# Hourglass attention with a ReGLU layer on one Trainium2 core: gate layer of chunks 2 to 5 in seven half products, in a new written order

## The chip, the cores and the metric

The kernel runs on one core of a Trainium2 chip. The core has engines that run their own instruction queues in order and meet at semaphores: TensorE (PE, matmuls, with weight loads shown apart as PEld), VectorE (DVE), ScalarE (ACT), GpSimd (POOL), and SyncE (SP), which here only starts transfers. The metric is the device time of one execution in microseconds (us). Before the change the median of three runs is 349.23 (348.65 to 349.43).

## The reference

Attention comes in two parts that are added, for 8 batches, 8 heads, 576 positions and head dimension 64; then a gated feed-forward layer follows, for 4608 tokens of 512 numbers, with 1536 inner columns:

```python
q_d, k_d, v_d = (t.reshape(B, H, S // 4, 4, D).mean(axis=3) for t in (q, k, v))
out = np.repeat(sm_attn(q_d, k_d, v_d), 4, axis=2)         # pooled 4:1
mask = np.abs(pos[:, None] - pos[None, :]) < 4
out += softmax(np.where(mask, scale * q @ k.T, -1e9)) @ v  # local band
x = out.transpose(0, 2, 1, 3).reshape(B * S, H * D)
y = (np.maximum(x @ w_gate, 0.0) * (x @ w_val)) @ w_out
```

## The kernel before

**Tiles.** The 64 heads are 32 head pairs, four to a batch; a pair fills the 128 partitions. Attention writes its output transposed into xT (four rows of 4608 columns in each partition, a row for each group of 128 of the 512 features). The feed-forward layer takes the tokens in 9 chunks of 512. A chunk's gate and value layers have 12 column blocks of 128 each; a block is four matmuls of 128x512 (emit_h_mm, L848), one for each row of xT, into one PSUM bank. ACT applies relu to a gate block (L857, into a ring r1 of three), and DVE multiplies it with the value block in PSUM (L860) into gT. PSUM has eight banks of 2 KB a partition, 512 numbers.

**The output layer in seven products.** The output layer of a chunk is done in two units of 256 tokens (class Unit, L904). A unit is a 2x2 block product in Strassen and Winograd's form: sums of blocks of gT on DVE (sums, L927, four of them, "next" being their low part and "sumhi" the high part), prepared combinations of weights (wt, L899), and seven products p/1 to p/7 of six matmuls of 128x256 each (mm, L933). Products accumulate in three PSUM regions a, b and d; ACT copies a out between them (keep, L967), and c11, c12, c22 on DVE and c21 on ACT give the results. p/7 adds to the region a, which keep/2 reads.

**Periods.** In the period of chunk c, the PE does the attention of four head pairs, the gate and value layers of chunk c, and the two units of chunk c-1. For a pair, the steps are the pooled and banded scores (L733, L737), exp on ACT (L746, L751), the mask on DVE (L759), denominators and numerators on PE (L764, L779, L784), the logarithm and the inverse on ACT (ln L796, inv L817), the normalization on DVE (xn, L799; L658 for early pairs), and the sum into xT (xsum, L803; L662 for early pairs). For pairs to come, q and k are loaded by POOL's DMAs (L365) and transposed by SP's (L426), keys are copied into block form on ACT (kk L696, kd L703), and keys and queries are pooled by DVE (pool, L433).

**The order is written by hand.** Each engine's queue has its instructions in the order of a list of tokens. A token names a step, its argument, its half period u, and its chunk: hg is a gate block, hv a value block, relu and gate what follows. FRONT covers the start and chunks 0 and 1; ORDER is one period, run for chunks 2 to 5 (emit_periods, L1299; "<" and ">" mean the chunk before or after); MAIN covers chunk 6, and then chunks 7 and 8, whose gate and value layers are also done in seven products: class Seven (L1081), its matmuls (product, L1094), copies (L1105) and finishing steps (L1110 on DVE, L1112 on ACT), the sums of weights (L1070) and of x (L1079), and a gate step that takes the maximum with zero itself (L1166). In chunks 2 to 5 the gate and value blocks use two pairs of PSUM banks in turn, 0 to 3, which they share with the units; attention has banks 4 to 7.

Of the kernel before, what the change touches and what calls it, by code (L numbers as in the profile page):

```python
# [9 lines left out]
FP32 = mybir.dt.float32  # L10
# [7 lines left out]
FRONT = """  # L18
pads loadk/0 loadv/0 loadq/1 loadk/1 loadv/1 loadq/2 cast tr/0/2/4 loadk/2 ev/0/20V/4 tr/0/1/3 tr/0/0/2
ev/0/21V/4 ev/0/10A/3 vd/0/6 loadv/2 ev/0/11A/3 ev/0/01A/2 ev/0/00A/2 loadq/3 warm/5/6 tr/1/0/7 vc/0/6  # L20
s1/0/2 ev/1/00A/7 loadk/3 tr/1/2/1 ed/0/2 tr/1/1/0 ev/1/20V/1 ev/1/11A/0 loadv/3 sd/0/6 ev/1/21V/1
ev/1/10A/0 rd/0/6 ex/0/0/2 td/0/6 wg/0 brief/16/2 vd/1/6 ev/1/01A/7 warm/2/7 ma/0/0 ex/0/1/2 s1/1/0 wv/0
ma/0/1 ed/1/0 ones/4 su/0/4 ex/1/1/0 ru/0/4 loadq/4 ex/1/0/0 tu/0/0/4 warm/5/7 tr/2/1/2 tr/2/2/3 tu/0/1/4
ev/2/11A/2 tr/2/0/0 ev/2/10A/2 loadk/4 ev/2/21V/3 xp/0/0/4 ev/2/20V/3 ev/2/01A/0 xp/0/1/5 ev/2/00A/0
ma/1/0 loadv/4 vc/1/6 warm/1/7 s1/2/0 ma/1/1 xe/0/0A/4 xe/0/1V/5 sd/1/6 ex/2/1/0 ones/5 su/1/4 rd/1/6
td/1/6 ed/2/0 ru/1/4 warm/3/7 vd/2/6 loadq/5 tu/1/1/4 ex/2/0/0 tr/3/1/2 tu/1/0/4 tr/3/2/3 loadk/5 vc/2/6
tr/3/0/0 ev/3/20V/3 ev/3/10A/2 xp/1/1/5 sd/2/6 ev/3/21V/3 loadv/5 ev/3/01A/0 xe/1/1V/5 xp/1/0/4
ev/3/00A/0 ma/2/0 ev/3/11A/2 ma/2/1 xe/1/0A/4 s1/3/0 wg/1 rd/2/6 su/2/4 td/2/6 ed/3/0 ru/2/4 ex/3/0/0
tu/2/1/4 hv/0/0/7 wv/1 hv/0/1/7 tu/2/0/4 ex/3/1/0 vd/3/6 ma/3/0 ones/6 warm/4/1 const/0 const/1 xp/2/1/5
vc/3/6 xp/2/0/4 ma/3/1 sd/3/6 xe/2/1V/5 xe/2/0A/4 loadq/6 tr/4/0/0 rd/3/6 su/3/4 td/3/6 tr/4/1/2 loadk/6  # L30
ru/3/4 hv/1/0/1 ev/4/11A/2 tu/3/0/4 hg/0/0/6 ev/4/10A/2 hg/0/1/6 tu/3/1/4 loadv/6 tr/4/2/3 ev/4/01A/0
ev/4/00A/0 xp/3/1/5 ev/4/21V/3 ev/4/20V/3 xp/3/0/4 wg/2 hv/0/2/7 xe/3/1V/5 xe/3/0A/4 hg/1/0/0 s1/4/2 wv/2
hv/0/3/7 ex/4/0/2 hv/1/1/1 loadq/7 hg/1/1/0 hg/1/2/0 ed/4/2 ma/4/0 hv/1/2/1 hg/0/2/6 hg/0/3/6 ex/4/1/2
hg/1/3/0 hv/1/3/1 relu/0/6 tr/5/0/2 ma/4/1 tr/5/1/3 loadk/7 relu/1/0 tr/5/2/4 den/4/1/5 ev/5/20V/4 vd/4/6
ev/5/10A/3 hg/3/*/0 ev/5/21V/4 gate/0/7 vc/4/6 ev/5/00A/2 gate/1/1 hg/2/*/6 ev/5/11A/3 loadv/7 ev/5/01A/2
relu/3/0 den/4/0/4 relu/2/6 hv/2/*/7 wg/3 ln/4 num/4/0/2 wv/3 gate/2/7 tr/6/1/0 inv vd/5/1 num/4/1/3
loadq/8 s1/5/4 vc/5/1 xn/2 hv/3/*/1 ex/5/0/4 ev/6/11V/0 ed/5/4 ma/5/0 hg/4/*/2 gate/3/1 ex/5/1/4 loadk/8
tr/6/0/4 relu/4/2 ma/5/1 tr/6/2/1 hg/5/*/6 ev/6/20V/1 ev/6/00A/4 ev/6/01V/4 ev/6/10A/0 ev/6/21V/1
den/5/0/4 xsum/4 wo/0 den/5/1/5 num/5/0/2 ln/4 hv/4/*/3 wo/1 inv hv/5/*/7 gate/4/3 wo/2 relu/5/6 hg/6/*/0
gate/5/7 qk/b0/0@0 num/5/1/3 zero/b/5 relu/6/0 vd/6/1 xn/2 s1/6/4 vc/6/1 tr/7/1/0 ex/6/1/4 hv/6/*/1  # L40
ed/6/4 qk/b1/0@0 ma/6/1 hg/7/*/2 ex/6/0/4 hg/8/*/6 ma/6/0 relu/7/2 gate/6/1 qk/b2/0@0 tr/7/0/4 num/6/0/2
ev/7/01V/4 ev/7/00A/4 den/6/1/5 tr/7/2/1 qk/b3/0@0 ev/7/10A/0 den/6/0/4 ev/7/20V/1 hv/7/*/3 relu/8/6
ev/7/21V/1 xsum/5 wo/3 ln/4 hv/8/*/7 gate/7/3 inv vd/7/1 ev/7/11V/0 gate/8/7 num/6/1/3 zero/b/6 vc/7/1
hg/9/*/0 loadv/8 xn/2 s1/7/4 relu/9/0 xsum/6 hg/10/*/2 ex/7/0/4 wt/0 v/b/0@0 ex/7/1/4 hv/10/*/3 ma/7/0
relu/10/2 ma/7/1 hv/9/*/1 ed/7/4 gate/10/3 qk/a0/1@0 hg/11/*/0 gate/9/1 qk/a1/1@0 next/0/1@0 den/7/0/4
relu/11/0 tr/8/1/2 qk/a2/1@0 den/7/1/5 flip/9 zero/k/0 ev/8/11V/2 tr/8/2/3 ev/8/10A/2 next/1/1@0 tr/8/0/0
qk/a3/1@0 hv/11/*/1 ln/4 ev/8/01V/0 ev/8/20V/3 v/a/1@0 ev/8/21V/3 inv num/7/0/6 gate/11/1 num/7/1/7
zero/b/0 p/1/0@1 qk/b0/1@0 ev/8/00A/0 sumhi/0/0@1 xn/6 p/2/0@1 keep/1/0@1 qk/b1/1@0 vd/8/1 xsum/7
scores/a/0@1 vc/8/1 qk/b2/1@0 sumhi/1/0@1 wt/1 vd/9/1 exp/a1/0@1 hg/0/0@1 qk/b3/1@0 ed/a/0@1 c11//0@1
v/b/1@0 sum/2/0@1 p/6/0@1 vc/9/1 relu/0/0@1 wt/2 p/5/0@1 v4/b/1@0 exp/a0/0@1 flip/10 hv/0/0@1 mask/a1/0@1  # L50
keep/2/0@1 qk/a0/0@1 mask/a0/0@1 p/7/0@1 gate/0/0@1 o/a00/0@1 sum/3/0@1 keep/3/0@1 o/a01/0@1 qk/a1/0@1
o/a10/0@1 ln/a0/0@1 o/a11/0@1 c22//0@1 hg/2/0@1 zero/b/1 wt/3 qk/a2/0@1 ln/a1/0@1 p/3/0@1 qk/a3/0@1
pool/b/0@1 inv/a/0@1 p/4/0@1 v/a/0@1 hv/2/0@1 c21//0@1 c12//0@1 v4/a/0@1 relu/2/0@1 xn/a0/0@1 hg/1/0@1
xn/a1/0@1 hv/1/0@1 relu/1/0@1 qk/b0/0@1 flip/11 xsum/a/0@1 scores/b/0@1 gate/1/0@1 hg/3/0@1 exp/b1/0@1
qk/b1/0@1 next/0/0@1 exp/b0/0@1 qk/b2/0@1 hg/4/0@1 mask/b1/0@1 ed/b/0@1 mask/b0/0@1 qk/b3/0@1 hv/3/0@1
next/1/0@1 tn/1/0@1 v2/b/0@1 v4/b/0@1 relu/3/0@1 gate/2/0@1 relu/4/0@1 o/b00/0@1 o/b01/0@1 gate/3/0@1
o/b10/0@1 ln/b0/0@1 o/b11/0@1 vd/10/0 pool/a/0@1 v/b/0@1 p/1/1@1 ln/b1/0@1 hg/5/0@1 inv/b/0@1 flip/12
hv/5/0@1 qk/a0/1@1 keep/1/1@1 xn/b1/0@1 qk/a1/1@1 p/6/1@1 xn/b0/0@1 zero/b/2 zero/v/0 hv/4/0@1 qk/a2/1@1
keep/2/1@1 next/2/0@1 vc/10/0 zero/d/0 qk/a3/1@1 scores/a/1@1 relu/5/0@1 gate/4/0@1 p/7/1@1 v/a/1@1
exp/a0/1@1 gate/5/0@1 p/2/1@1 exp/a1/1@1 mask/a0/1@1 hg/0/1@1 ed/a/1@1 mask/a1/1@1 xsum/b/0@1 keep/3/1@1  # L60
qk/b0/1@1 o/a00/1@1 relu/0/1@1 o/a01/1@1 c11//1@1 o/a10/1@1 o/a11/1@1 next/3/0@1 tn/3/0@1 v1/a/1@1
v2/a/1@1 v4/a/1@1 flip/13 p/4/1@1 ln/a1/1@1 qk/b1/1@1 pool/b/1@1 p/5/1@1 ln/a0/1@1 hg/2/1@1 inv/a/1@1
c22//1@1 hv/0/1@1 c21//1@1 xn/a0/1@1 hg/1/1@1 xn/a1/1@1 zero/b/3 zero/v/1 const/2 p/3/1@1 relu/1/1@1
gate/0/1@1 qk/b2/1@1 scores/b/1@1 c12//1@1 hg/3/1@1 qk/b3/1@1 exp/b1/1@1 xsum/a/1@1 exp/b0/1@1 flip/14
mask/b1/1@1 qk/a0/0@2 hv/1/1@1 ed/b/1@1 mask/b0/1@1 tm/b/1@1 v1/b/1@1 v2/b/1@1 v4/b/1@1 qk/a1/0@2
hv/2/1@1 gate/1/1@1 relu/3/1@1 kk/a0/1@1 kk/a1/1@1 pool/a/1@1 relu/2/1@1 o/b00/1@1 o/b01/1@1 o/b10/1@1
ln/b0/1@1 o/b11/1@1 hv/3/1@1 v/b/1@1 ln/b1/1@1 hg/5/1@1 gate/3/1@1 qk/a2/0@2 inv/b/1@1 kd/a0/1@1
kd/a1/1@1 gate/2/1@1 zero/d/1 hg/4/1@1 xn/b1/1@1 hv/4/1@1 relu/4/1@1 xn/b0/1@1 zero/b/4 zero/v/2 zero/k/1
relu/5/1@1 qk/a3/0@2 hv/5/1@1 xsum/b/1@1 qk/b0/0@2 qk/b1/0@2 qk/b2/0@2 qk/b3/0@2 v/a/0@2 v/b/0@2
"""  # L70
MAIN = """
fl/31 o:scores/a/0@6 o:gate/5/1@5 o:p/1/0@6 o:exp/a0/0@6 o:gate/4/1@5 o:hg/0/0@6 o:sumhi/0/0@6 o:ed/a/0@6
o:mask/a0/0@6 o:p/2/0@6 o:relu/0/0@6 o:kk/b0/0@6 o:kk/b1/0@6 o:sumhi/1/0@6 o:next/0/1@5 o:o/a00/0@6
o:keep/1/0@6 o:o/a01/0@6 o:o/a10/0@6 o:next/1/1@5 o:o/a11/0@6 o:hg/2/0@6 o:pool/b/0@6 o:ln/a0/0@6
o:p/6/0@6 o:c11//0@6 o:hv/0/0@6 o:sum/2/0@6 o:keep/2/0@6 o:inv/a/0@6 o:kd/b0/0@6 o:kd/b1/0@6 o:sum/3/0@6
o:p/5/0@6 o:relu/2/0@6 o:after/3/0@6 o:v1/a/0@6 o:v2/a/0@6 o:v4/a/0@6 o:xn/a0/0@6 o:p/7/0@6 o:hg/4/0@6
o:keep/3/0@6 o:p/4/0@6 o:next/0/0@6 o:c22//0@6 o:scores/b/0@6 o:gate/0/0@6 o:c21//0@6 o:p/3/0@6
o:exp/b0/0@6 o:next/1/0@6 o:hv/2/0@6 o:c12//0@6 o:ed/b/0@6 o:mask/b0/0@6 o:tm/b/0@6 o:v1/b/0@6 o:v2/b/0@6
o:v4/b/0@6 oy/0/0 o:hg/1/0@6 o:gate/2/0@6 o:o/b00/0@6 o:o/b01/0@6 o:next/3/0@6 o:relu/1/0@6 o:o/b10/0@6
o:o/b11/0@6 o:pool/a/0@6 o:hv/1/0@6 o:ln/b0/0@6 o:hv/4/0@6 o:gate/1/0@6 o:inv/b/0@6 o:kd/a0/0@6  # L80
o:kd/a1/0@6 o:kk/a1/0@6 o:hg/3/0@6 o:xsum/a/0@6 o:relu/4/0@6 o:kk/a0/0@6 o:xn/b0/0@6 o:hv/3/0@6
o:relu/3/0@6 o:p/1/1@6 o:hg/5/0@6 wv/0 o:keep/1/1@6 o:gate/3/0@6 o:scores/a/1@6 o:relu/5/0@6 o:p/6/1@6
o:next/2/0@6 o:exp/a0/1@6 o:gate/4/0@6 o:hg/0/1@6 o:mask/a0/1@6 o:tm/a/1@6 o:v1/a/1@6 o:v2/a/1@6
o:v4/a/1@6 o:keep/2/1@6 o:hv/5/0@6 o:ed/a/1@6 o:kk/b0/1@6 ws/0 o:relu/0/1@6 o:p/7/1@6 o:gate/5/0@6
o:o/a00/1@6 o:o/a01/1@6 o:xsum/b/0@6 o:keep/3/1@6 o:kk/b1/1@6 o:o/a10/1@6 o:o/a11/1@6 o:ln/a0/1@6
o:hg/2/1@6 o:pool/b/1@6 o:p/2/1@6 o:inv/a/1@6 o:kd/b0/1@6 o:kd/b1/1@6 o:p/4/1@6 o:c11//1@6 o:hv/0/1@6
o:xn/a0/1@6 o:c21//1@6 o:p/5/1@6 o:hg/1/1@6 o:c22//1@6 ws/2 oy/1/1 o:scores/b/1@6 o:relu/1/1@6 oy/0/1
o:p/3/1@6 o:gate/0/1@6 o:exp/b0/1@6 o:hg/3/1@6 o:mask/b0/1@6 o:ed/b/1@6 o:hv/2/1@6 o:relu/2/1@6
# [49 lines left out]
ORDER = """  # L138
# [1262 lines left out]
```

## Time and profile before

| | |
|---|---|
| median of three runs | 349.23 us (349.23, 349.43, 348.65) |
| the profiled execution | 348.82 us |
| its span in the trace | 347.1 us |
| granted clock of TensorE, mean | 1.00 |
| busy: DVE / ACT / POOL | 270.1 / 257.4 / 184.0 us |
| periods of chunks 2, 3, 4, 5 | 37.60, 36.06, 36.06, 35.40 us |

The span is the time between the first and the last instruction that the profiler shows; the execution's own time is 1.7 us longer. A group of instructions is written as line, engine, operation, output <- input, shapes and count, then busy time, mean duration in ns, and the idle time just ahead with what ended it. In a timeline a row is start, duration, and what ran, with the idle time ahead in brackets. Durations overlap in a stream: a matmul's row of 379 ns and the next one's start 216 ns after its own. The marks of the periods are the starts of the first pair's pooled scores.

### The profile page before, as it was taken

How to read it: one execution, taken by the hardware profiler on the slowest of the kernel's cores; microseconds unless marked ns; L12 is line 12 of the kernel's file. 1: busy time of each engine (PE TensorE's matmuls, PEld its weight loads, DVE VectorE, ACT ScalarE, POOL GpSimd, SP SyncE). 2: the span in 40 equal slices, each digit the busy share in tenths (PEclk: the TensorE clock that was granted, in tenths of full speed). 3: DMA queues.
4: the chain of work that ended last, by engine and by line, in shares of the span. 5: the costliest groups of instructions: out<-in, count | busy, mean ns of one | idle time of the engine just before them, and what ended most of it. 6: DMA issues, size and time to landing. Idle time of an engine off the chain costs nothing.

```text
span 347.1 us, 8449 instructions
## 1 busy us (share of the span) xinstructions
PE 337.0 (97%) x3230; PEld 226.7 (65%) x3230; DVE 270.1 (78%) x509; ACT 257.4 (74%) x548; POOL 184.0 (53%) x267
## 2 busy tenths in 40 slices
PE   8899999999989999999999999999999999999996
PEld 4765556656565656666566657665656668888875
DVE  5694769899888777777777778776887898897692
ACT  3878778878886887688777877787777647896842
POOL 8995557777839995977678876822222000000000
PEclk9999999999999999999999999999999999999999
DMA  9999999999999999999969999996000102002013
GB/s 136 166 171 192 186 192 162 145 188 150 204 131 140 190 186 178 176 174 141 179 100 169 161 170 95 191 148 133 2 31 2 63 0 93 1 17 93 16 54 129
DMA packets 162172, 43.87 MB, mean 126 GB/s; under 512 B 147500, under 2 KB 156820, under 8 KB 162132
## 3 DMA queue, kind: packets, MB, share of 16 engines
q0 software_dynamic: 123136, 19.51, 82.0%
q1 hardware_dynamic: 38884, 23.80, 35.4%
q8 instruction: 25, 0.41, 0.5%
q14 instruction: 15, 0.12, 0.2%
q10 hardware_dynamic: 112, 0.02, 0.0%
HBM read 46.59 MB, written 9.44 MB: 161 GB/s over the span
## 4 chain that ended last, share of the span: by engine, by line
PE 77%; ACT 14%; DVE 3%; DMA 2%; issue 2%; SPq 0%; ACTq 0%; DVEq 0%
PE ps L848 33%; PE ps L1094 17%; PE ps L933 12%; ACT r L857 2%; DMA out_dram<-y_sb 2%; ACT kk L696 2%; ACT rden L817 2%; PE ps L1018 2%; PE ps L764 2%; PE ps L446 2%; PE ps L737 1%; PE ps L784 1%; PE ps L779 1%; ACT rden L796 1%; ACT cst_sb L703 1%
## 5 line engine op out<-in xcount | busy, mean ns | idle before, releaser
L848 PE MATMUL ps<-xT,wg_sb 128*128 128x512 f16 x344 | 86.4, 379 | 3.0 <-ACT r L857 2.1
L848 PE MATMUL ps<-xT,wv_sb 128*128 128x512 f16 x352 | 88.4, 379 | 0.0
L860 DVE TENSOR_TENSOR gT<-r,ps 128x512 f16<-128x512 f16 x84 | 56.2, 682 | 20.2 <-PE ps L848 15.5
L857 ACT ACTIVATE r<-ps 128x512 f16<-128x512 f32 x84 | 50.0, 599 | 26.2 <-PE ps L848 22.1
L848 PEld LDWEIGHTS <-wg_sb 128*128 128x128 f16 x344 | 32.0, 97 | 35.9 <-issue 6.0
L848 PEld LDWEIGHTS <-wv_sb 128*128 128x128 f16 x352 | 32.7, 98 | 33.7
L365 POOL DMA_DIRECT2D qk<-in_k_dram x46 | 33.4, 732 | 10.9 <-DMA qk<-in_q_dram 9.4
L365 POOL DMA_DIRECT2D qk<-in_q_dram x46 | 33.9, 743 | 5.5 <-DMA qk<-in_k_dram 1.6
L933 PEld LDWEIGHTS <-xo 128*128 128x128 f16 x288 | 27.3, 98 | 7.9 <-issue 0.4
L433 DVE TENSOR_REDUCE qkd<-qkT 128x288 f16<-128x1152 f16 x23 | 30.9, 1343 | 0.0
L383 POOL DMA_DIRECT2D vw<-in_v_dram x40 | 29.1, 740 | 1.4 <-PE ps L933 1.3
L933 PE MATMUL ps<-wt,xo 128*128 128x256 f16 x216 | 27.8, 272 | 0.1
L1105 ACT COPY ps<-ps 128x256 f32<-128x256 f32 x54 | 19.3, 366 | 8.9 <-PE ps L1094 7.6
L933 PEld LDWEIGHTS <-gT 128*128 128x128 f16 x216 | 20.8, 98 | 7.0 <-issue 0.4
L478 POOL TENSOR_TENSOR vd<-v 48x192 f16<-48x192 f32 x40 | 23.8, 595 | 1.5
L759 DVE TENSOR_TENSOR att<-att,zero_sb 128x576 f16<-128x576 f16 x20 | 9.8, 490 | 17.6 <-ACT att L746 17.3
L817 ACT ACTIVATE rden<-rden 128x720 f32<-128x720 f32 x28 | 22.5, 803 | 0.9
L470 POOL TENSOR_TENSOR v<-v 112x384 f32<-112x384 f32 (+1 forms) x21 | 21.5, 1025 | 1.5
L967 ACT COPY q<-ps 128x256 f32<-128x256 f32 x36 | 13.3, 370 | 11.8 <-PE ps L933 11.4
L799 DVE TENSOR_TENSOR xn<-ps,rden 128x720 f16<-128x720 f32 x20 | 18.0, 902 | 1.3 <-ACT rden L817 0.7
L933 PE MATMUL ps<-wo_sb,gT 128*128 128x256 f16 x144 | 18.8, 273 | 0.1
L1292 POOL COPY seen<-att 112x1 f16<-112x1 f16 x15 | 3.7, 246 | 25.6 <-DVE att L759 22.3
(156 smaller groups left out, 732.3 us busy)
## 6 DMA issues: line engine op xcount, KB each, us to landing
out_dram<-y_sb SPq DMA_DIRECT2D x24, 256.0 KB, 4.6
v<-in_v_dram SPq DMA_DIRECT2D x20, 192.0 KB, 4.1
qk<-in_q_dram POOLq DMA_DIRECT2D x46, 72.0 KB, 6.1
qk<-in_k_dram POOLq DMA_DIRECT2D x46, 72.0 KB, 6.9
vw<-in_v_dram POOLq DMA_DIRECT2D x38, 80.0 KB, 7.2
v<-in_v_dram SPq DMA_DIRECT2D x20, 144.0 KB, 5.9
out_dram<-y_sb SPq DMA_DIRECT2D x22, 128.0 KB, 1.8
vw<-in_v_dram POOLq DMA_DIRECT2D x12, 168.0 KB, 7.7
```

The lines of the kernel that those rows point to most:

```text
L365: nc.gpsimd.dma_start(dst.rearrange("p (j h d) -> p j h d", h=2, d=64)[:, :, hh, :], _dap(src, off + hh * S * D, [[D, 96], [NQ * D, NB], [ ...
L383: nc.gpsimd.dma_start(t[lo : lo + 64, j0:j1, lo : lo + 64], _dap(v, base + j0 * QB * D, [[D, 64], [QB * D, j1 - j0], [1, D]]),)
L433: nc.vector.tensor_reduce(out=qkd[hp % 2].rearrange("p i t -> p (i t)"), in_=qkT[hp % 4][:, 0 : 2 * S].rearrange("p (t f) -> p t f", f=4), ...
L470: nc.gpsimd.tensor_tensor(out=m, in0=t[:, :, 0:128], in1=t[:, :, 128:256], op=ALU.add)
L478: nc.gpsimd.tensor_tensor(out=vp[hp % 3][lo : lo + 48, :, lo : lo + 64], in0=m[:, :, 0:64], in1=m[:, :, 64:128], op=ALU.add)
L817: nc.scalar.activation(out=rden, in_=rden, func=AF.Exp, scale=-1.0)
L848: nc.tensor.matmul(out=out, lhsT=w[:, kk, bass.ts(jj, 128)], rhs=xT[:, kk, c * TCH : (c + 1) * TCH], start=(kk == 0), stop=(kk == 3),)
L857: nc.scalar.activation(out=r1[j % 3], in_=h1, func=AF.Relu)
L860: nc.vector.tensor_tensor(out=gT[c % 2][:, jj, :], in0=r1[j % 3], in1=h2, op=ALU.mult)
L933: nc.tensor.matmul(out=out, lhsT=left[:, i, :], rhs=right[i], start=(first and i == 0), stop=(i == NK - 1), skip_group_check=True,)
L1094: nc.tensor.matmul(out=out, lhsT=self.left[i][t], rhs=self.right[i][t], start=(i == 1 and t == 0), stop=(t == n - 1), skip_group_check=True,)
L1105: nc.scalar.copy(out=o, in_=a)
```

## The change: chunks 2 to 5

**Pairs of gate blocks.** In chunks 2 to 5, the gate blocks j and j+6, for j from 0 to 3, are computed together as a 2x2 block product (two column blocks by two halves of 256 tokens, with the 512 features split in two). It takes seven products of two matmuls of 128x256, 14 in place of eight of 128x512. The blocks 4, 5, 10 and 11 stay as they were (gh, followed by the relu rl). A new class does the pairs:

```diff
+    def emit_xq(c, i):
+        (b11, b12), (b21, b22) = [[x_half(c, k, n) for n in range(2)] for k in range(2)]
+        t1, t2, t3, t4 = x_sums(c)
+        o, a, b = ((t1, b12, b11), (t2, b22, t1), (t3, b22, b12), (t4, b21, t2))[i]
+        nc.vector.tensor_tensor(out=o, in0=a, in1=b, op=ALU.subtract)
+
+    class Gate7:
+        def __init__(self, c, j, bank, tile):
+            self.a, self.e, self.b, self.d = (
+                ps[:, bank + i // 2, 256 * (i % 2) : 256 * (i % 2) + 256] for i in range(4)
+            )
+            self.t = tg[tile : tile + 2]
+            self.m = xT[:, j % 2, (6 if c < 4 else 3) * TCH :][:, 0:TCH].bitcast(FP32)
...
+        def product(self, i):
+            out = (self.a, self.d, self.b, self.a, self.e, self.a, self.a)[i - 1]
+            for k in range(2):
+                nc.tensor.matmul(
+                    out=out,
+                    lhsT=self.left[i - 1][:, k, :],
+                    rhs=self.right[i - 1][:, k, :],
+                    start=(i == 1 and k == 0),
+                    stop=(k == 1),
+                    skip_group_check=True,
+                )
+
+        def copy(self, i):
+            o, x = {1: (self.d, self.a), 2: (self.b, self.a), 5: (self.m, self.e)}[i]
+            nc.scalar.copy(out=o, in_=x)
+
+        def finish(self, i):
+            o = self.t[i // 10 - 1][:, 256 * (i % 10) - 256 : 256 * (i % 10)]
+            if i % 10 == 1:
+                nc.scalar.copy(out=o, in_=self.d if i == 11 else self.a)
+            else:
+                nc.vector.tensor_tensor(out=o, in0=self.b if i == 12 else self.a, in1=self.m, op=ALU.add)
```

Its tokens are sq (a product, L1276), sk (an ACT copy, L1287) and sf (a finishing step: 11 and 21 on ACT, L1292; 12 and 22 on DVE, L1294). The text sq/0.0.2.5 is pair 0, PSUM bank 0, tile 2, product 5. A pair uses two banks: A and E lie in one, B and D in the next. The number m, a copy of E, lies in xT, in row 0 or 1 (that of j modulo 2), in the columns of chunk 6 (for chunks 2 and 3) or of chunk 3 (for 4 and 5). The x differences (xq, L1257, four a chunk) lie in the columns of chunk 7 or 2, and the sums of weights (zs, L1251, two sets of four, made once) in those of chunks 8 and 1: columns that hold no x at that time.

**The gate.** All twelve blocks of these chunks use one DVE instruction that takes the maximum with zero and multiplies (gt, L1320), so the pairs need no relu.

**The order.** FRONT, ORDER and MAIN become one written list, SEQ. The set zs/0 stands in the front between gate/11 of chunk 0 and the normalization xn/6 of a head pair; the set zs/1 stands at the end of chunk 1, ahead of gate/5. The periods have a new order throughout, and value blocks (vh) and plain gate blocks name their PSUM bank. They now use banks 4 to 7 too. POOL's and SP's instructions and transfers are the same in another order. The period of chunk 3 begins:

```
gh/4.7/0@3 kk/b0/0@3 xq/0/0@3 rl/4.7.0/0@3 gt/11.3.1/1@2 xq/1/0@3 sumhi/0/0@3 scores/a/0@3 exp/a0/0@3 p/1/0@3
ed/a/0@3 qk/b0/0@4 next/0/1@2 sq/0.0.2.1/0@3 kk/b1/0@3 sumhi/1/0@3 sk/0.0.2.1/0@3 gh/5.6/0@3 rl/5.6.3/0@3
vh/5.4/0@3 sq/0.0.2.2/0@3 keep/1/0@3 v1/a/0@3 next/1/1@2 gt/5.4.3/0@3 sq/0.0.2.5/0@3 mask/a0/0@3 sum/2/0@3
pool/b/0@3 vh/4.6/0@3 gt/4.6.0/0@3 sq/0.0.2.6/0@3 kk/a1/0@3 p/6/0@3 xq/2/0@3 o/a00/0@3 sum/3/0@3 v2/a/0@3
sk/0.0.2.5/0@3 qk/a2/1@3 sf/0.0.2.11/0@3 o/a01/0@3 v4/a/0@3 sk/0.0.2.2/0@3 o/a11/0@3 p/2/0@3 ln/a0/0@3 qk/a3/0@4
keep/2/0@3 p/5/0@3 kd/b0/0@3 qk/a3/1@3 c11//0@3 kd/b1/0@3 p/7/0@3 keep/3/0@3 scores/b/0@3 c22//0@3
```

**A start flag.** A unit's product p/5 no longer opens its region itself; p/2, which comes before it in the same bank, does:

```diff
         def p5(self):
-            self.mm(self.b, self.s1, wt[0], True)
+            self.mm(self.b, self.s1, wt[0], False)
```

Chunks 6 to 8 keep their tokens in their order, written with "t:" where they came from MAIN. Most lines of the kernel after are 71 further down than before.

## The prediction

> **What bounds the kernel now.** I read the page first (busy time by engine, then the chain that ended last), then the windows of the four periods that run chunks 2 to 5, the PE's waits and timeline in them, and the groups of instructions kept apart by shape.
>
> ```profile
> PE 337.0 (97%) x3230; PEld 226.7 (65%) x3230; DVE 270.1 (78%) x509; ACT 257.4 (74%) x548; POOL 184.0 (53%) x267
> ...
> PE 77%; ACT 14%; DVE 3%; DMA 2%; issue 2%; SPq 0%; ACTq 0%; DVEq 0%
> ...
> L433 DVE TENSOR_REDUCE qkd<-qkT 128x288 f16<-128x1152 f16 x23 | 30.9, 1343 | 0.0
> ```
>
> PE is busy 97% of the span and carries 77% of the chain. The windows (columns: stretch, length, then busy time of PE, weight loads, DVE, ACT, POOL with instruction counts, granted clock, DMA share, GB/s) cut the span at the pooled-score matmuls that open each period, with a stretch of the late layers last:
>
> ```profile
> 96.85:134.45 37.60, 36.02 (x310) 22.93 (x308) 29.18 (x47) 28.83 (x55) 31.54 (x47) 1.00 1.74 160
> 134.45:170.51 36.06, 35.87 (x311) 22.86 (x308) 27.14 (x45) 27.82 (x52) 26.73 (x41) 1.00 1.47 174
> 170.51:206.57 36.06, 35.87 (x311) 22.87 (x308) 27.15 (x45) 27.83 (x52) 27.65 (x42) 1.00 1.57 149
> 206.57:241.97 35.40, 35.21 (x304) 22.27 (x302) 26.77 (x44) 27.82 (x52) 17.81 (x28) 1.00 1.19 143
> 280.00:300.00 20.00, 20.00 (x172) 16.64 (x170) 18.38 (x41) 14.02 (x43) 0.00 (x0) 1.00 0.12 40
> ```
>
> Periods 3 to 5 leave PE 0.19 us idle each; period 2 leaves 1.58, nearly all in two waits for relu:
>
> ```profile
> 98.32 1.02 PE L848 MATMUL ps<-xT,wg_sb 128*128 128x512 f16 x4 [0.84 <-ACT r L857]
> ...
> 115.50 1.02 PE L848 MATMUL ps<-xT,wg_sb 128*128 128x512 f16 x4 [0.68 <-ACT r L857]
> ```
>
> So PE work that is removed is time, and any new wait of PE is time as well. Durations of operations of the added kinds, from the seven-product layers of chunks 7 and 8 (after the line's shape: count, busy time, mean ns):
>
> ```profile
> L1094 PE MATMUL ps<-xT,wg_sb 128*128 128x256 f16 x66 | 11.9, 273 | 0.0
> L1105 ACT COPY ps<-ps 128x256 f32<-128x256 f32 x54 | 19.3, 366 | 8.9 <-PE ps L1094 7.6 <-DVE y_sb L1110 0.4
> L1166 DVE SCALAR_TENSOR_TENSOR gT<-r,ps 128x512 f16<-128x512 f16 x3 | 2.0, 682 | 0.0
> L1110 DVE TENSOR_TENSOR r<-ps,vw 128x256 f16<-128x256 f32 x16 | 6.6, 417 | 0.1
> L1112 ACT CAST r<-ps 128x256 f16<-128x256 f32 x16 | 5.7, 388 | 0.2
> L1079 DVE TENSOR_TENSOR xT<-xT 128x512 f16<-128x512 f16 x8 | 3.3, 416 | 0.0
> ```
>
> These durations overlap in a stream. From start to start in the timeline, independent operations take less: matmul 128x512 0.216 us, 128x256 0.109; gate 0.61; copy and cast 0.27; PSUM add and x difference 0.335; mask 0.38; 768-wide sum 0.47; pool reduction 1.27; relu 0.53. Handoffs between engines take 0.03 to 0.11.
>
> **1. Matmuls taken out.** Per pair, 8 x 0.216 = 1.73 becomes 14 x 0.109 = 1.53: 0.20 less. Four pairs in each of four chunks: 16 x 0.202 = **-3.23**. The count rises by 16 x 6 = 96, and the built program has just that, so the change does what it says.
>
> **2. Old waits that go.** Gate tokens no longer alternate in two PSUM pairs, and relu is called a third as often in the period. The 0.135 + 0.033 in each of periods 3 to 5 goes: -0.50. In period 2 the 0.68 and 0.03 go: -0.71. The wait at its start stays in another form: the new first gate block needs all of chunk 2's x, whose last sum (L662) ends at 97.62, and loses 1.19 where 1.35 was lost: -0.16. What is late next here is that sum, not relu.
>
> **3. Weight sums in front (zs/0).** Four DVE adds of 0.335 are queued ahead of an attention normalization, which had 0.30 of slack around it:
>
> ```profile
> 59.20 0.91 DVE L658 TENSOR_TENSOR xn<-ps,rden 128x720 f16<-128x720 f32 x1 [0.21 <-ACT rden L817]
> ...
> 60.95 0.95 DVE L899 TENSOR_TENSOR wt<-wo_sb,wt 128x1536 f16<-128x1536 f16 x1
> ```
>
> Everything behind is 1.34 - 0.30 = 1.04 later, wt/1 among it: it ends at 62.94 in place of 61.90, and PE, due at p/6 at 62.28, gets it at 62.99: **+0.70**. At worst the whole 1.34, at best 0 (other PE work between).
>
> **4. A wait the diff doesn't show.** In the semaphore waits of the built program, ACT's copy sk/5 of the first pair (E to m, L1287) waits for PE in all four chunks, and in chunks 2 and 3 for DVE as well: for the x difference xq/2 (L1257). No data passes between them. xq/2 reads two rows of xT, 4608 columns each, as one strided operand: for chunk 2 from column 1280 of row 0 to column 1535 of row 1. Counted as one address range this encloses m, at row 0, columns 3072 to 3583. For chunks 4 and 5, m is at 1536, ahead of the range. That explains the pattern; whatever its cause, the wait is in the program.
>
> What it costs in chunk 3, from the start of the last matmul of vh/5.4. DVE and ACT, each behind the other: matmul and handoff 0.43, gt/5.4 0.61, mask 0.38, sum/2 0.47, pool 1.27, gt/4.6 0.61, xq/2 0.46 with handoff, sk/5 0.27, sf/11 0.39 (to its end, since sk/2 waits for that), sk/2 0.27, ln 0.67, keep/2 0.42 = 6.25. PE issues meanwhile, until p/7, which overwrites what keep/2 reads: 0.22 + sq/2 0.22 + sq/5 0.22 + vh/4.6 0.86 + sq/6 0.22 + p/6 0.66 + attention outputs 0.38 + 0.25 + 0.15 + p/2 0.66 + p/5 0.66 = 4.50. PE stands **1.75**. Queued behind sk/5 on ACT are sf/11, sk/2, ln and keep/2; kd, keep/3 and inv follow. Bounds: 0, if the order gives more cover than I count, and 2.0, if every operation takes its full duration at a handoff. I take 1.75, since all terms have rows of their own kind.
>
> In chunk 2 DVE is late besides: zs/1's four adds stand behind the sum at 97.62, so gt/5.4 starts at 97.62 + 1.34 + two gates 1.21 + two differences 0.67 + four sums 1.2 = 102.0, while PE has vh/5.4 ready at 101.2. 1.75 + 0.80 = **2.55** (0 to 2.9).
>
> In chunks 4 and 5 the same chain without the DVE wait leaves 0.1 us or more to spare.
>
> **5. Load on the other engines.** DVE gains per period 8 adds into the tiles and 4 differences, 12 x 0.335 = 4.0: 31.2 of some 35.2 us. ACT gains per pair 5 x 0.27 less 2 x 0.53, 0.28: 28.9 of 35.2. Neither becomes the bound: in the last window above DVE is busy 18.38 of 20.00 (92%) with the same kinds of operation, and PE 20.00. I take 0.05 a period for handoffs that come late, **+0.20** (0 to 3.1, priced under C). POOL and SP issue the same instructions and DMAs in another order; POOL is busy 26.7 of 36 and no wait of PE for a load stands in these periods, so that order costs nothing; if a load came late, its wait would show on the transposed q and k (L426, L433).
>
> One rule of the Trainium skill speaks against the layout. That last window ran at full PE occupancy with the sub-results A and E in one PSUM bank. The Trainium skill, Perfetto Trace Analysis, Matmuls (under Optimizing Tensor Performance), says that independent matmul groups should rotate through different banks, so that one is emptied while the next is filled; the change keeps A with E and B with D. By that rule the copies would hold PE up, as in C; by the row they don't, and the trace decides.
>
> **Sum:** -3.23 - 0.50 - 0.71 - 0.16 = -4.60; 0.70 + 2.55 + 1.75 + 0.20 = +5.20; together +0.60. The profiled execution took 348.82 (span 347.1 and 1.7 around it), so 349.4; the median of the three runs is 0.41 above it, 349.23, so **349.8**. A measurement of this kernel tells 0.2% (0.7 us) from no change; this is 0.57.
>
> **Rivals.**
> A, the forecast, 349.8, own range 348.7 to 350.9 (the stalls 0.70, 2.55 and 1.75 each off by a third, independently, are 1.1 either way). Chance 0.62: 0.06 faster, 0.34 same, 0.22 slower.
> B, faster: the wait of step 4 is covered, because xq/2 is done by the time sk/5 is due. Then 4.30 of the sum goes and 349.8 becomes 345.5. Against it: pool and two gates, 2.5 us, stand ahead of xq/2. For it: those ops wait in the trace of before as often as they run. Chance 0.16.
> C, slower: the half products are paced by ACT. Three of a pair's products overwrite A after an ACT copy of it (sk/1, sk/2) or need E or D copied in time; with ACT at 82% each pair may wait once or more. It decides as soon as a copy starts more than 0.1 us after its product. At 0.135, the wait for relu at 151.56, three times in 16 pairs is 6.5 at most; half of it, 3.1 beyond A, gives 352.9. Against it: the 20.00 of 20.00. Chance 0.17.
> D, slower: PE's clock falls in the stalls of step 4. The first fourteen matmuls (L1018, 128x512) started 427 ns apart against 216 later, so a cold stretch of that length, 14 matmuls, costs 14 x 0.21 = 2.9: 352.7. Against it: stalls of 1.35 and 0.84 stand in this trace and the granted clock is 1.00 in every window. Chance 0.05. The Trainium skill, TensorE: Matmul & The Clock Gate, HAM oscillation — how this bites in real kernels, puts the limit at idle gaps of some 3.4 us, longer than any stall here; the trace has no such gap in its periods to show it.
>
> **Chances.** Faster 0.06 + 0.16 = 0.22; within 0.2% 0.34; slower 0.22 + 0.17 + 0.05 = 0.44. Cases of both signs are likely, so the range spans B too: 345.2 to 352.7, outside of which lie a third of B and half of C and D, some 0.16.
>
> **What would show it.** Right: PE idle of some 1.7 us ahead of p/7 (the matmul L1004 reading s3) in period 3, some 2.5 in period 2, released by the copy keep (L1038), and none there in periods 4 and 5; the pool reduction and two gates ahead of xq/2 in DVE's timeline; in front, L1004 at 62.3 some 0.7 late. Period 4 should be near 36.06 - 0.81 - 0.17 = 35.1 long. Wrong: those gaps absent (B); small gaps ahead of every half product, released by L1287 (C); granted clock under 1.00 in period 2 (D).

## The result, and the profile after

The changed kernel takes 350.4 us in the median of 15 runs (349.57 to 352.83), the kernel before 348.73 us in 15 runs beside it. The ratio is 1.0054 (95% interval 1.0035 to 1.0072), which makes 1.9 us slower; the two medians are 1.67 apart. Five of the 15 runs show a granted clock of 0.99 to 0.995 and take about 1.9 us more than the other ten; the last section comes back to them. The forecast was 349.8 within 345.2 to 352.7, with slower as the likeliest side.

The page of the changed kernel, its engines, its chain, and one group of PE; below it the same group of the kernel before:

```profile
PE 334.3 (96%) x3326; PEld 235.9 (68%) x3326; DVE 291.1 (83%) x565; ACT 260.1 (75%) x596; POOL 186.0 (53%) x267
...
PE 76%; ACT 13%; DVE 4%; DMA 3%; issue 2%; POOL 0%; DVEq 0%; ACTq 0%; POOLq 0%
...
L1004 PE MATMUL ps<-wt,xo 128*128 128x256 f16 x216 | 28.8, 272 | 4.0 <-ACT q L1038 3.8
```

```profile
L933 PE MATMUL ps<-wt,xo 128*128 128x256 f16 x216 | 27.8, 272 | 0.1
```

PE has 2.7 us less work in the records and a longer span (348.6 after 347.1). The last two lines say where it went: the unit's products waited 3.8 us in sum for ACT's copy keep (L1038), where the same group of before waited 0.1. The windows of the four periods of the changed kernel (marks: first scores of each; columns as in the prediction) say in which periods:

```profile
98.70:137.12 38.42, 35.73 (x333) 25.17 (x332) 34.69 (x62) 29.19 (x66) 30.86 (x46) 1.00 1.80 144
137.12:174.33 37.21, 35.10 (x333) 25.12 (x332) 31.05 (x57) 28.41 (x64) 26.47 (x40) 1.00 1.52 148
174.33:209.41 35.08, 34.91 (x333) 25.23 (x332) 31.89 (x56) 28.50 (x64) 29.62 (x44) 1.00 1.56 161
209.41:243.63 34.22, 34.05 (x330) 24.80 (x329) 31.69 (x56) 27.89 (x63) 17.32 (x26) 1.00 1.32 153
```

Periods 4 and 5 are 0.98 and 1.18 us shorter than before, periods 2 and 3 are 0.82 and 1.15 longer, with less PE work in all four. The long waits of PE in its timeline, in periods 2 and 3, and then one of the short ones, in the second half of period 3:

```profile
108.66 0.82 PE L1004 MATMUL ps<-wt,xo 128*128 128x256 f16 x6 [1.89 <-ACT q L1038]
```

```profile
146.56 0.81 PE L1004 MATMUL ps<-wt,xo 128*128 128x256 f16 x6 [1.95 <-ACT q L1038]
```

```profile
164.89 0.81 PE L1004 MATMUL ps<-xT,gT 128*128 128x256 f16 x6 [0.16 <-ACT q L1038]
```

The first two are p/7 of the first unit in chunks 2 and 3. Chunks 4 and 5 have no such wait ahead of p/7; the short ones of 0.16 stand ahead of p/4 in the second half of periods 3, 4 and 5. Behind keep, ACT's own timeline in period 3 shows what it waited for:

```profile
144.52 0.37 ACT L1287 COPY xT<-ps 128x256 f32<-128x256 f32 x1 [2.94 <-DVE xT L1257]
144.79 0.38 ACT L1292 CAST r<-ps 128x256 f16<-128x256 f32 x1
145.20 0.36 ACT L1287 COPY ps<-ps 128x256 f32<-128x256 f32 x1
145.47 0.78 ACT L867 ACTIVATE rden<-ps 128x720 f32<-128x720 f32 x1
146.13 0.38 ACT L1038 COPY q<-ps 128x256 f32<-128x256 f32 x1
```

The copy sk/5 stood 2.94 us for the x difference xq/2 (L1257), and then ACT did what was queued: sf/11, sk/2, the logarithm, keep/2. PE began p/7 at 146.56, 0.43 after the start of keep/2. DVE, which made the copy wait, was not idle:

```profile
140.60 0.69 DVE L1320 SCALAR_TENSOR_TENSOR gT<-xT,ps 128x512 f16<-128x512 f16 x1 [1.16 <-ACT xT L1318]
141.20 0.57 DVE L830 TENSOR_TENSOR att<-att,zero_sb 128x576 f16<-128x576 f16 x1
141.69 0.54 DVE L998 TENSOR_TENSOR xo<-gT 128x768 f16<-128x768 f16 x1
142.16 1.34 DVE L504 TENSOR_REDUCE qkd<-qkT 128x288 f16<-128x1152 f16 x1
143.42 0.67 DVE L1320 SCALAR_TENSOR_TENSOR gT<-r,ps 128x512 f16<-128x512 f16 x1
144.02 0.41 DVE L1257 TENSOR_TENSOR xT<-xT 128x512 f16<-128x512 f16 x1
```

It is the chain of the prediction, operation by operation: gate, mask, sum, pool, gate, xq/2.

**Where the time went.** A bracket in the timeline counts from a matmul's modelled end. A matmul of 128x256 lasts 272 ns and the next may start after 109, so a wait costs its bracket and 0.16 more. Counted from start to start, against the spacing of each shape, PE loses:

| place | before | after | change | forecast |
|---|---|---|---|---|
| front, up to the first gate blocks of chunk 1 | | | +0.78 | +0.70 |
| start of chunk 2 | 1.31 | 1.83 | +0.52 | -0.16 |
| ahead of p/7 in chunks 2 and 3 | 0 | 4.17 (2.05 and 2.12) | +4.17 | +4.30 |
| old waits in the periods | 3.27 | 0 | -3.27 | -1.21 |
| new short waits in the periods | 0 | 1.80 | +1.80 | +0.20 |
| ahead of a value block at 124.78 | 0 | 0.84 | +0.84 | 0 |
| work (what is left of the span's +1.5) | | | -3.34 | -3.23 |

### The profile page after: what moved, and what is told of

The parts are those of the page before. It is cut to its first block, busy times and chain, and to the rows that moved or that the text cites. A ratio compares the mean times of both kernels' runs of the same rounds, so it can differ in the third digit from the quotient of the medians.

```text
span 348.6 us, 8787 instructions
## 1 busy us (share of the span) xinstructions
PE 334.3 (96%) x3326; PEld 235.9 (68%) x3326; DVE 291.1 (83%) x565; ACT 260.1 (75%) x596; POOL 186.0 (53%) x267
## 4 chain that ended last, share of the span: by engine, by line
PE 76%; ACT 13%; DVE 4%; DMA 3%; issue 2%; POOL 0%; DVEq 0%; ACTq 0%; POOLq 0%
PE ps L919 29%; PE ps L1165 17%; PE ps L1004 11%; PE ps L1276 6%; PE ps L835 2%; DMA out_dram<-y_sb 2%; PE ps L855 2%; DMA vw<-in_v_dram 1%; ACT q L1038 1%; PE ps L850 1%; PE ps L808 1%; ACT cst_sb L774 1%; PE ps L517 1%; ACT rden L888 1%; ACT kk L767 1%
## 5 line engine op out<-in xcount | busy, mean ns | idle before, releaser
L919 PE MATMUL ps<-xT,wg_sb 128*128 128x512 f16 x216 | 55.1, 379 | 1.8 <-DVE xT L733 0.9
L919 PEld LDWEIGHTS <-wv_sb 128*128 128x128 f16 x352 | 33.5, 98 | 32.8 <-issue 1.4
L919 PEld LDWEIGHTS <-wg_sb 128*128 128x128 f16 x216 | 20.1, 97 | 20.3 <-issue 1.9
L1004 PE MATMUL ps<-wt,xo 128*128 128x256 f16 x216 | 28.8, 272 | 4.0 <-ACT q L1038 3.8
L931 DVE TENSOR_TENSOR gT<-r,ps 128x512 f16<-128x512 f16 x36 | 24.2, 683 | 7.0 <-PE ps L919 3.7
L928 ACT ACTIVATE r<-ps 128x512 f16<-128x512 f32 x36 | 21.2, 598 | 8.9 <-PE ps L919 8.7
L549 POOL TENSOR_TENSOR vd<-v 48x192 f16<-48x192 f32 x40 | 25.4, 636 | 1.7
L867 ACT ACTIVATE rden<-ps 128x720 f32<-128x720 f32 x20 | 15.4, 772 | 10.6 <-PE ps L850 10.6
L1320 DVE SCALAR_TENSOR_TENSOR gT<-r,ps 128x512 f16<-128x512 f16 x32 | 21.3, 680 | 1.4 <-PE ps L919 1.4
L1276 PE MATMUL ps<-xT 128*128 128x256 f16 x128 | 21.6, 272 | 0.0
```

Source lines behind the costliest of these rows:

```text
L549: nc.gpsimd.tensor_tensor(out=vp[hp % 3][lo : lo + 48, :, lo : lo + 64], in0=m[:, :, 0:64], in1=m[:, :, 64:128], op=ALU.add)
L919: nc.tensor.matmul(out=out, lhsT=w[:, kk, bass.ts(jj, 128)], rhs=xT[:, kk, c * TCH : (c + 1) * TCH], start=(kk == 0), stop=(kk == 3),)
L931: nc.vector.tensor_tensor(out=gT[c % 2][:, jj, :], in0=r1[j % 3], in1=h2, op=ALU.mult)
L1004: nc.tensor.matmul(out=out, lhsT=left[:, i, :], rhs=right[i], start=(first and i == 0), stop=(i == NK - 1), skip_group_check=True,)
L1276: nc.tensor.matmul(out=out, lhsT=self.left[i - 1][:, k, :], rhs=self.right[i - 1][:, k, :], start=(i == 1 and k == 0), stop=(k == 1), skip ...
L1320: lambda c, jj, b, t: nc.vector.scalar_tensor_tensor(out=gT[c % 2][:, jj, :], in0=tg[t], scalar=0.0, in1=ps[:, b, :], op0=ALU.max, op1=ALU ...
```

## The experiments

Each is the changed kernel with one edit, unless it says more. "Before" ran beside each; its median was 348.56 to 348.81. The theory is the one of the forecast: a wait between two operations that share no data, made by where m lies. The main rival: ACT and DVE are simply late with the added copies and additions.

**1. m out of the range.**

```diff
-            self.m = xT[:, j % 2, (6 if c < 4 else 3) * TCH :][:, 0:TCH].bitcast(FP32)
+            self.m = xT[:, j % 2 * 2 + 1 if c < 4 else j % 2, (6 if c < 4 else 3) * TCH :][:, 0:TCH].bitcast(FP32)
```

> The number m of chunks 2 and 3 is moved to rows 1 and 3 of xT, out of the address range that xq/2 spans; order and work are the same. Forecast's theory (the copy sk/5 is held by xq/2, and p/7 behind it): the two stalls of 2.05 and 2.12 us ahead of p/7 go, and chunks 2 and 3 keep only the small ones that chunks 4 and 5 show (about 0.5 each): some 3.2 us faster than the changed kernel, 347.2. Rival (ACT and DVE are simply late with the added copies and adds, and the wait only shows it): the stalls stay within 1 us of their size, 349.4 or more.

345.83 us against 348.81, ratio 0.9914 (0.9897 to 0.993): 3.0 us faster than before, and 4.9 faster than the changed kernel by the two ratios. In the waits of its PE between 95 and 250 us (total, times, longest) the unit's products are down to four short ones; the other line is the wait for the last x at the start of chunk 2:

```profile
PE ps L919 <- DVE xT L733: 0.9, 1, 0.9
PE ps L1004 <- ACT q L1038: 0.6, 4, 0.2
```

No operation was taken out and no token moved, so the stalls came from the place of m alone; the rival falls. I had expected 347.2, since I gave chunks 2 and 3 the 0.48 of short waits in exchange; those stand in the second half of a period, and chunk 3 had them already. All 4.17 went, and the 0.84 at 124.78 did not come up either.

**2. m into the range, in chunk 4.**

```diff
-            self.m = xT[:, j % 2, (6 if c < 4 else 3) * TCH :][:, 0:TCH].bitcast(FP32)
+            self.m = xT[:, j % 2, (6 if c < 4 else 7 if c == 4 else 3) * TCH :][:, 0:TCH].bitcast(FP32)
```

> The number m of chunk 4 is moved to the columns of chunk 7, where the range of that chunk's xq/2 encloses it; chunks 2, 3 and 5 as in the changed kernel. Forecast's theory: a third stall of 1.6 to 2.0 us appears ahead of p/7 in chunk 4, 352.1. Rival (chunks 2 and 3 are special for another reason, such as loads or the start of the periods): no stall in chunk 4, 350.4.

352.35 us, ratio 1.0109 (1.0089 to 1.0129), 1.9 above the changed kernel. PE's timeline, and ACT's, in chunk 4 of this kernel:

```profile
183.24 0.81 PE L1004 MATMUL ps<-wt,xo 128*128 128x256 f16 x6 [2.21 <-ACT q L1038]
```

```profile
181.20 0.37 ACT L1287 COPY xT<-ps 128x256 f32<-128x256 f32 x1 [3.19 <-DVE xT L1257]
```

The third stall is there, 2.37 us from start to start, in a period that had none, so chunks 2 and 3 need no other reason than the address. With the first experiment this shows that the wait follows the place of m against the range that xq/2 spans, and that each such wait costs PE 2.05 to 2.37 us here.

**3. xq/2 earlier, the wait kept.** In chunks 2 and 3 the token is moved ahead of the pool reduction:

```diff
-keep/1/0@3 v1/a/0@3 next/1/1@2 gt/5.4.3/0@3 sq/0.0.2.5/0@3 mask/a0/0@3 sum/2/0@3 pool/b/0@3 vh/4.6/0@3 gt/4.6.0/0@3
-sq/0.0.2.6/0@3 kk/a1/0@3 p/6/0@3 xq/2/0@3 o/a00/0@3 sum/3/0@3 v2/a/0@3 sk/0.0.2.5/0@3 qk/a2/1@3 sf/0.0.2.11/0@3
+keep/1/0@3 v1/a/0@3 next/1/1@2 gt/5.4.3/0@3 sq/0.0.2.5/0@3 mask/a0/0@3 sum/2/0@3 xq/2/0@3 pool/b/0@3 vh/4.6/0@3 gt/4.6.0/0@3
+sq/0.0.2.6/0@3 kk/a1/0@3 p/6/0@3 o/a00/0@3 sum/3/0@3 v2/a/0@3 sk/0.0.2.5/0@3 qk/a2/1@3 sf/0.0.2.11/0@3
```

> In chunks 2 and 3 the x difference xq/2 stands ahead of the pool reduction in the written order; the wait of sk/5 on it stays. Forecast's theory: xq/2 ends 1.27 + 0.61 us earlier, the stall of chunk 3 falls from 2.1 to 0.5 or less and that of chunk 2 from 2.05 to 0.5 or less, some 3.2 us faster, 347.2. Rival (late ACT): no gain, and the pool reduction 0.33 later, 350.4 to 351.

346.06 us, ratio 0.9922 (0.9904 to 0.994). ACT still waits for xq/2, but not for long, in chunk 2:

```profile
104.32 0.37 ACT L1287 COPY xT<-ps 128x256 f32<-128x256 f32 x1 [1.00 <-DVE xT L1257]
```

PE's losses ahead of p/7 are 0.20 and 0.38 in place of 2.05 and 2.12. So the price of the wait is the queue ahead of xq/2 on DVE, as the sum of step 4 had it.

**4. zs/0 out of the front.** Two of its four additions go ahead of xn/b1/0@1, one ahead of xn/a0/1@1, one ahead of xn/b1/1@1, where DVE stood 0.73, 0.66 and 0.85 us for ACT.

> The four weight sums zs/0 leave the front and stand in three idle stretches of DVE in chunk 1 (ahead of normalizations that wait for ACT). Forecast's theory: PE's delay in the front, 0.7 to 0.78 us, is gone, 349.7. Rival (the front's delay is made up later, or the sums make the same delay in chunk 1): 350.4.

349.73 us, ratio 1.0031 (1.0013 to 1.0049): 0.8 below the changed kernel by the ratios. The two intervals overlap, so the times alone don't tell theory from rival; the trace does: p/6 in front starts at 62.17 in place of 63.06, and the gate block that comes at 70.20 in the changed kernel comes at 69.31 (before: 69.42). The front's delay was not made up later; step 3 holds.

**5. No POOL additions in the periods.** In the profile after I had found something that the forecast lacked. DVE operations on two operands in SBUF sometimes took far longer than others of their shape, 15 of them by 0.24 to 0.84 us, each beside work of POOL. (In the kernel before there were three.) On the kernel of experiment 1, the steps v1 and v2 are skipped in chunks 2 to 5.

> The kernel of the experiment with m in rows 1 and 3, without POOL's additions of v (L541, L549) in the periods of chunks 2 to 5: this part of the pooled values is left out. In the profiles after the change some 15 additions and subtractions of DVE take 0.15 to 0.84 us longer than others of their shape, each beside POOL's work. Theory (POOL's additions stretch them): most of the 15 are gone, those beside POOL's transfer issues stay. As PE has no stall that they cause in that kernel, the time stays within 0.5 of 345.8. Rival (DVE is the hidden bound and the stretching paces PE): 1 us or more faster, 344.8 or less.

345.47 us, ratio 0.9908 (0.9893 to 0.9923), the same as experiment 1 within the intervals. All stretched operations in the periods are gone, those too that I had put down to transfer issues: 60 operations with two operands in SBUF still ran beside such issues in these periods, and none was stretched. One sum of the same place, in experiment 1 and then in this kernel:

```profile
124.57 0.84 DVE L998 TENSOR_TENSOR xo<-gT,xo 128x768 f16<-128x768 f16 x1
```

```profile
124.48 0.55 DVE L998 TENSOR_TENSOR xo<-gT,xo 128x768 f16<-128x768 f16 x1
```

So POOL's additions stretch them, and in experiment 1 this costs nothing that can be measured.

**6. POOL's additions where they were.** The kernel of experiment 1, with the additions of each half period behind a small POOL copy that waits for DVE's mask or sum (tm, after), as before the change: for example "mask/b0/0 tm/b/0 v1/b/0 v2/b/0" in place of v1/b far ahead of the mask.

> The kernel with m in rows 1 and 3, and POOL's additions of v placed behind a small copy that waits for a DVE step, as in the kernel before. Theory (the old order kept POOL's additions beside DVE's reductions and PSUM reads; the new order lost that): fewer and shorter stretched DVE operations, 3 to 8 in place of 15. Time within 0.5 of 345.8, since nothing that ends the path waits on them. Rival (the stretching doesn't depend on the place): 15 as before.

346.05 us, ratio 0.9924 (0.9909 to 0.9938). The stretched operations fall from 15 to 11 and are all sums (L998) now; their extra time falls from 6.4 to 4.0 us. That is less than I had expected (3 to 8), and the time is the same within the intervals.

**7. The other stalls.** On the kernel of experiment 1: zs/0 as in experiment 4; in chunk 2, p/1 and the first scores ahead of the first gate block; in each period's second half, ed/a right behind exp/a0 and keep/3 ahead of kd/a1.

> m in rows 1 and 3; zs/0 in idle stretches of DVE in chunk 1; in chunk 2, p/1 and the first scores ahead of the first gate block, which waits for the last x; in the second half of each period the pooled exp and the copy keep/3 one or two places earlier on ACT. Each is meant to take a stall seen in the profiles: 0.75 in front, up to 1.1 at the start of chunk 2, 0.48 in each period. Theory (each stall is local, PE bounds the rest): 345.8 - 0.75 - 1.0 - 1.7 = 342.4. Rival (other handoffs are nearly as late, so half of it comes back): 344.

344.2 us, ratio 0.9871 (0.9856 to 0.9886): nearer to the rival. The short waits of the second halves are gone from PE's timeline in all four periods (1.95 us from start to start in experiment 1). At the start of chunk 2 most came back one step later:

```profile
101.33 1.02 PE L919 MATMUL ps<-xT,wv_sb 128*128 128x512 f16 x4 [0.81 <-ACT att L822]
```

And one of the moved weight sums lasted 2.00 us in place of 0.42, beside POOL's additions; the normalization behind it was late, and PE lost some 0.9 us at 88 us. Here a stretched operation did cost time.

**8. The same with POOL as in experiment 6.**

> The kernel before this one in the list with POOL's additions behind waits for DVE steps as well. Theory (stretched DVE operations cost PE nothing where it has slack): the same time within 0.5, with fewer stretched operations. Rival (POOL waits longer and loads come late): 0.5 to 2 us slower, with PE idle ahead of the scores.

343.74 us, ratio 0.987 (0.9849 to 0.9891). No difference from experiment 7 that the intervals can tell; the loss at 88 us did not come up, and PE waited for no load. The other half of the theory failed: the profile has 18 operations stretched by 0.15 us or more, where experiment 7's has 13. So the place behind DVE's steps is no cure for the stretching, in spite of experiment 6.

**9. Both exps first in chunk 2.** On the kernel of experiment 8, exp/a0/0@2 and ed/a/0@2 stand ahead of kk/b0/0@2 on ACT.

> The last kernel of the experiments before (m moved, zs/0 later, scores first in chunk 2, pooled exp and keep/3 earlier, POOL's additions behind DVE), with both exps of chunk 2's first pair ahead of the key copy and the relu on ACT. In that kernel PE loses 0.97 us at 100.66 to the pooled exp, which stands behind a relu that waits for the late first gate block. Theory (local stall): 0.7 to 0.9 faster, 342.9. Rival (the gate block's bank or the relu is nearly as late): 343.5 to 343.8.

343.28 us, ratio 0.9846 (0.9824 to 0.9869): below the rival's 343.5 to 343.8, but nearer to it than to 342.9, and not to be told from experiment 8 by the intervals. PE's wait only moved on, to the next ACT copy: 1.11 us from start to start at 101.58, released by sk (L1287). It has the lowest median of the versions tried, some 5.4 us below before.

I had put this lateness down to a relu that waits for the late first gate block. ACT's timeline of the changed kernel doesn't bear that out:

```profile
98.97 0.71 ACT L767 COPY att<-qkT 64x640 f16<-64x640 f16 x1
99.58 0.59 ACT L1318 ACTIVATE r<-ps 128x512 f16<-128x512 f32 x1
100.07 0.63 ACT L817 ACTIVATE att<-ps 128x576 f16<-128x576 f32 x1
100.60 0.52 ACT L822 ACTIVATE att<-ps 128x432 f16<-128x432 f32 x1
```

The relu (99.58) comes right behind a key copy, 0.7 us after the gate block ended (98.86), and no row of ACT from 96 to 103 us has idle time ahead of it, here and in experiments 7, 8 and 9. So PE waits there for an ACT that has more queued than it can do, and moving one step only changes for which it waits. No run takes work off ACT in this stretch, so what that would bring stays open.

## Why the prediction held, and where it didn't

**Right: step 4, the term that decides the sign.** Forecast 4.30, measured 4.17. The parts were off against each other, so that the close sum is in part luck, and the 2.12 of chunk 3 lies beyond the upper bound of 2.0 that step 4 gave. Chunk 2 was forecast at 2.55 and lost 2.05: DVE reached its gate 0.56 late, not 0.80. Chunk 3 was forecast at 1.75 and lost 2.12: its gate waited 0.18 longer, for the relu on ACT, its mask took 0.12 longer, and the rest is spread. The cause, inferred from four waits of the built program, held in experiments 1 and 2, and the queue on DVE that sets its price in experiment 3.

**Right: steps 1 and 3.** Work -3.34 (forecast -3.23), front +0.78 (+0.70). Period 4 was forecast at 35.1 and is 35.08 long, but that is luck: its old waits cost 0.68 in place of the 0.17 that was taken off, and new ones of 0.49 came in.

**Wrong in size: step 2, the old waits.** I took the bracket of the timeline, 0.135 and 0.033, as PE's loss. From start to start the three waits of a steady period cost 0.68, not 0.17, and those of chunk 2 come to 1.23, not 0.71. The same slip made the new waits of step 5 look small: what is 0.16 in a bracket is 0.32 of time. Old waits were undersized by 2.06 and new ones by 1.60, so that most of both slips cancelled.

**Wrong: the start of chunk 2.** Forecast -0.16, measured +0.52. The wait for the last x is as forecast (1.10 from start to start). I had not followed ACT behind it: its queue is full there, and PE loses 0.60 more to the pooled exp (0.26), the copy sk (0.15) and the second relu (0.19), each ended just ahead of the block that waited. Experiments 7 and 9 show how that lateness moves from one ACT step to the next.

**Wrong: POOL's order costs nothing (step 5).** I had looked at loads alone. In the profile after, POOL's additions run beside a sum into xT and stretch it from 0.75 to 1.59 us; the normalization behind it is late, and PE loses 0.84:

```profile
122.12 1.59 DVE L874 TENSOR_TENSOR xT<-xn 128x576 f16<-128x576 f16 x1
123.82 0.91 DVE L870 TENSOR_TENSOR xn<-ps,rden 128x720 f16<-128x720 f32 x1
```

```profile
124.78 1.89 PE L919 MATMUL ps<-xT,wv_sb 128*128 128x512 f16 x8 [0.68 <-DVE xn L870]
```

It wasn't there in the profiles of experiments 1 to 4. Those of 2 to 4 have a lesser one each (0.37 to 0.52), at another place: a stretched sum, a finishing step of DVE behind it, and a product that waits for that step. So where it strikes differs from profile to profile, and the new order allows it. The forecast was 0.9 too low for the profiled execution: 0.68 and 0.84 too little in these last two points, 0.46 too much in the sizes of the short waits, 0.16 in the other terms. Over all runs the change of 1.9 us is three times the 0.57 of the forecast; the ten runs at full clock lie 1.2 above the kernel before (349.9 against 348.73), so the lower clock of the other five has a part in the rest.

**The rivals.** B (the wait is covered) is what experiment 1 built: 345.83, where B had 345.5. C (ACT paces the half products) did not come about: PE's losses in periods 4 and 5 are 0.49 each, and experiment 7 took most of these. In the four periods two half products start late, both in period 2: one by 0.15 behind ACT's copy sk, one by 0.13 behind a finishing step of DVE. The rule from Perfetto Trace Analysis, Matmuls, of the Trainium skill, that independent groups rotate through different banks, finds little support in this trace: A shares its bank with E, and at most those 0.28 could be put down to that. D (the clock) may have come about in part, in a third of the runs, as the last section tells. Its price was misread: the trace of before has 427 ns between the first twelve matmuls, not fourteen, which makes 2.3 in place of 2.9. Nor does the granted clock of 1.00 in every window speak against it, since the column also gives 1.00 for the first 5 us, where nine of these stand. In the profiled execution it is the rows behind the stalls that do: the six matmuls of p/7 take 0.82 and 0.81 us, as six of their shape do elsewhere (p/4: 0.81).

## What to carry to other kernels

Read the built program's waits against those that the data ask for: a strided operand over two rows counts here as everything between its first and last element, so a copy into a scratch buffer in unused columns of a shared tile can wait on an operation that it has nothing to do with; moving the buffer to other rows was worth 4.9 us, 4.17 of it the two stalls of the profile. Size a wait from start to start, not by the bracket. After taking a wait out, look at the queue behind the late operation; here the same lateness came up at its next member.

## What the runs showed of the hardware that was not expected

**POOL's additions stretch DVE's.** In experiment 1's profile 15 DVE operations are 0.15 to 0.84 us longer than the median of their shape, all with two SBUF operands (L998, L1257, L830, L874); none that reads PSUM and no reduction of one operand is. In its periods, 28 operations with two SBUF operands overlap an addition of POOL, and 12 of them are stretched (two more stretched ones have only transfer issues beside them, and one lies outside the periods); of 50 that read PSUM beside an addition none is. Without POOL's additions in the periods no stretched one is left there (experiment 5). GPSIMD Engine Reference of the Trainium skill, 1. Specifications, has the SBUF interfaces of GpSimd shared with VectorE, with contention for DVE instructions that have two SBUF inputs. The runs agree, up to 1.58 us on an operation of 0.42 (experiment 7).

**Stalls of 2 us and the granted clock.** Each run lists its mean granted clock. With p/7's stalls in the kernel (the changed one, experiments 2 and 4), 10 of 31 runs show 0.989 to 0.995, the others 0.998 or more. Without them (experiments 1, 3, 5 to 9), none of 31 does. The kernel before, whose longest wait in the periods is 1.00 from start to start, shows 0.995 in 4 of the 33 runs beside the experiments. In the changed kernel the five such runs have a median of 351.8, the other ten 349.9. A mean of 0.995 over 350 us is 1.75 us of clock lost (an estimate from these two figures), near the 1.9 by which those runs are longer. So in a third of its runs a kernel with these stalls loses more than the stalls' own length. That the clock falls in the stalls is not shown: the profiled executions all have 0.998 or more, and what is missing there lies at their very end (experiment 8: 0.84 from 338.00 to 341.50, where PE has 0.20 us of work left). TensorE: Matmul & The Clock Gate of the Trainium skill, HAM oscillation — how this bites in real kernels, names gaps of over some 3.4 us as what costs the clock; here kernels with gaps of 1.9 to 2.4 us show the lower clock in a third of their runs.
